# Constant matrix products in idle stretches of TensorE, in an attention and feed-forward kernel

## The chip, the cores and the metric

The kernel runs on one core of a Trainium2 chip. A core has TensorE (PE in the profile) for matrix products, with a queue of weight loads (PEld) beside it, VectorE (DVE), ScalarE (ACT), GpSimd (POOL) and SyncE (SP), which mostly issues DMA transfers. Each engine works off its own instructions in the order in which the program gives them, and waits for others through semaphores. The metric is the device time of one execution in microseconds (us); where several executions were timed, their median.

## The reference

Eight attention heads in each of four batches have 768 positions of width 64. Queries and keys are each assigned to one of 16 centroids of their head, and a query sees only keys of its own cluster. The result of all heads, 3072 rows of 512, goes through a feed-forward layer with a Mish activation.

```python
q_assign = np.argmax(np.einsum('bhsd,hcd->bhsc', q_n, c_n), axis=-1)
k_assign = np.argmax(np.einsum('bhsd,hcd->bhsc', k_n, c_n), axis=-1)
mask = q_assign[:, :, :, None] == k_assign[:, :, None, :]
scores = scale * np.matmul(q, k.transpose(0, 1, 3, 2))
scores = np.where(mask, scores, -1000000000.0)
...
attn = attn / (np.sum(attn, axis=-1, keepdims=True) + 1e-09)
return np.matmul(attn, v).astype(np.float32)
...
h = x @ w_in
g = h * np.tanh(sp)          # sp = log(1 + exp(h))
return (g @ w_out).astype(np.float32)
```

## The kernel before

**Units.** The attention is cut into 96 units: unit i is one head (i // 3 over all batches) and one block of 256 queries. Each unit has two halves a = 0, 1 of 128 queries, and all names carry both: `s12_0` is the score tile of unit 12, first half. Batch 0 is units 0 to 23 and runs in a single-precision form of its own; at the same time the weights of the feed-forward layer are loaded and split into two 16-bit halves (the tiles `w` and `stage`), so that VectorE, ScalarE and GpSimd are busier there than later. From about 175 us on, the feed-forward products of one batch run between the attention of the next.

**One half in batch 0.** `scores` makes s (128 x 768) by four products of width 384 in a tile of two PSUM banks, `[P, 2, 512]`, of which columns 384 to 511 of each bank stay unused: the spare columns. There are two such tiles (the pool `ps2`, tag "S"). `rowmax` reduces s on VectorE to m, `expo` writes p = exp(s + m) on ScalarE with the row sums l, `p_lo` transposes p on TensorE by six products with the identity into two PSUM tiles q, `ptrans` copies these to pt (one by ScalarE, one by VectorE), and `pv` multiplies by the values into o, with the inverse row sums spread by four more products. `pv_out` scales o: ScalarE makes rb, VectorE xf, ScalarE and GpSimd the two halves of x.

**Order.** Nothing is scheduled by the hardware or a compiler. The class `Plan` collects every operation with a time from the tables T and N, sorts them, and issues them in this order; `after` issues first what an operation needs. `tie` then fixes the order of each engine's instructions as issued. Semaphores come from a layer that tracks which instruction reads and writes which tile.

**Other work on TensorE.** `w_sq` makes Gram products of the weights (the tile `gram`, four 128-wide bf16 products per weight tile), `assign_mm` and `assign_put` belong to the centroids. `warm(n)` issues n products of width 512 of the constant tile `idle` (bf16, all ones) into a PSUM tile `wake` that nothing reads. It is called four times: 17 products at the start, 18 and 4 in the assignment of the first heads, and 5 behind the scores of unit 0.

**Operands of a head.** For each head, GpSimd and others prepare A, B, T and Z (`prep_hi`, `prep_lo`), and DMA transfers copy parts between them (`copy_a` and its kin) and put in the cluster rows (`hot_copy`). `scores` waits for the last of these before the first unit of a head.

Of the kernel before, what the change touches and what calls it, by code (L numbers as in the profile page):

```python
# [20 lines left out]
P = 128  # L21
# [50 lines left out]
def tile_clustered_attention_mish_ffn(  # L72
# [9 lines left out]
    nc = tc.nc  # L82
# [22 lines left out]
    pl = Plan(tc)  # L105


    idle = cp.tile([P, 512], BF16, name="idle")
# [3 lines left out]
    def warm(n):  # L112
        for _ in range(n):
            nc.tensor.matmul(wake, idle[:, :P], idle, start=True, stop=True)
# [3 lines left out]
    def share(n, key, late):  # L118

        f = T[key, int(late)]  # L120
        return int((n + 1) * f) != int(n * f)
# [98 lines left out]
    st = {}  # L220
# [387 lines left out]
        eng.dma_start(st["T", n][D : D + NCL].bitcast(F32), stg[r + NCL : r + 2 * NCL])  # L608


    def scores(i, a):
        g, qb, n = units[i]
        pl.after(*((nm, n) for nm in ("hot_copy", "copy_a", "copy_b")))
        q0 = qb * 256 + a * P
        s = ps2.tile([P, 2, 512], F32, tag="S", name=f"s{i}_{a}")
        for j in range(2):
            nc.tensor.matmul(  # L617
                s[:, j, :384], st["B", n][:, q0 : q0 + P], st["A", n][:, j * 384 : (j + 1) * 384],
                start=True, stop=False,
            )  # L620
        for j in range(2):
            nc.tensor.matmul(  # L622
                s[:, j, :384], st["T", n][: D + NCL, q0 : q0 + P],
                st["Z", n][: D + NCL, j * 384 : (j + 1) * 384],
                start=False, stop=True,
            )
        st["s", i, a] = s
        if i == 0 and a:
            warm(5)

    def rowmax(i, a):
        pl.after(("scores", i, a))
# [35 lines left out]
    def mode(i, a):  # L668


        n, late = 2 * i + a, i >= T["units0"]
        if i < T["wide"]:
            return 3
        return 2 if share(n, "f_lo", late) else int(share(n, "f_hi", late))
# [13 lines left out]
    def p_lo(i, a):  # L688
        pl.after(("p_hi", i, a))
        if mode(i, a) == 3:  # L690
            for c in range(6):
                if c % 3 == 0:
                    o = st["q", i, a, c // 3] = ps.tile([P, 512], F32, tag="H", name=f"q{i}_{a}_{c}", bufs=2)
                nc.tensor.transpose(o[:, c % 3 * P : (c % 3 + 1) * P], st["p", i, a][:, c * P : (c + 1) * P], ident)
            return
        t, p, r = st["hl", i, a], st["p", i, a], st["l", i, a]
        if mode(i, a) == 2:
            nc.gpsimd.tensor_scalar(p, p, r, 1.0, op0=ALU.mult, op1=ALU.mult)
            nc.gpsimd.tensor_tensor(t[:, 1], p, t[:, 0], op=ALU.subtract)
        else:  # L700
            nc.vector.scalar_tensor_tensor(t[:, 1], p, r, t[:, 0], op0=ALU.mult, op1=ALU.subtract)  # L701
# [166 lines left out]
    def ffn(j):  # L868
# [3 lines left out]
    ops = {  # L872
        fn.__name__: fn
        for fn in (scores, rowmax, expo, total, recip, p_hi, p_lo, ptrans, e_mish, e_gh, e_gl)
    }
    def start(i):
# [109 lines left out]
    for i in range(NU):  # L986
        for a in range(2):
            if mode(i, a) == 3:
                for key in ("scores", "rowmax", "expo", "recip"):
                    pl.at(start(i) + T[key, a], ops[key], i, a)  # L990
                pl.at(start(i) + T["recip", a] - 0.001, total, i, a)
                pl.at(start(i) + T["q_hi", a], p_hi, i, a)
                pl.at(start(i) + T["q_lo", a], p_lo, i, a)
                pl.at(start(i) + T["q_trans", a], ptrans, i, a)
            else:
                e = i // 2 * 2 + N["E"][i % 2 * 2 + a]
                for key in ("scores", "rowmax", "expo", "total", "recip", "p_hi", "p_lo", "ptrans"):
                    pl.at(e + N[key], ops[key], i, a)
        if i % 2:
            early = mode(i, 0) == 3  # L1000
            for part in range(3):
                pl.at(start(i) + T["pv"] + T["pv_step"] * part if early else i + N["pv"][part], pv, i // 2, part)
            for u in (i - 1, i):
                pl.at(start(i) + T["pv_out"] if early else i + N["pv_out"] + 0.1 * (u - i), pv_out, u)
                pl.at(start(i) + T["pv_out"] if early else i + N["x_lo"] + 0.1 * (u - i), x_lo, u)
# [215 lines left out]
```

## Time and profile before

| | |
|---|---|
| median of 3 executions | 915.11 us (913.28 to 915.86) |
| the profiled execution's own time | 913.7 us |
| its span from the first to the last instruction | 912.0 us |
| mean granted TensorE clock | 0.988 |
| busy: PE, DVE, ACT, POOL | 859.8, 648.3, 490.9, 427.6 us |
| PE busy from 0 to 215 us | 183.73 of 215 us, clock 0.95 |
| PE busy from 215 to 908 us | 675.86 of 693 us, clock 1.00 |
| DVE busy from 0 to 215 us | 175.45 of 215 us |

A row of the timeline gives the start and the busy time in us, engine, line, operation, output and inputs, how many instructions are merged, and in brackets the idle time of the engine just before with what ended it. A row of the table by stage gives a stretch, its length, the busy time of an engine (with its instructions), the granted TensorE clock as a share of full speed, the busy share of the DMA engines and what they moved. Ends of matrix products are modelled, so a step from one start to the next says more about their price than the busy time.

### The profile page before, as it was taken

The page shows a single profiled execution, that of the slowest core. Times are in us where ns is not written, and L with a number is a line of the kernel's source. Part 1 is how long each engine was busy: PE and PEld are TensorE (multiplying, and loading weights), DVE is VectorE, ACT ScalarE, POOL GpSimd, SP SyncE. Part 2 cuts the span into 40 slices and gives each one's busy share as a digit, 9 for nine tenths or more (in the row PEclk, how much of TensorE's full clock was granted, in tenths as well). Part 3 has the DMA queues.
Part 4 walks back from the last instruction along what each step waited for, and adds up shares of the span by engine and source line. Part 5 has one row for each costly group of instructions (what it writes and reads, how often), then busy time and mean ns, then how long its engine had stood idle before and what let it go on. Part 6 is the DMA issues. An engine that isn't in the chain of part 4 may idle for free.

```text
span 912.0 us, 16959 instructions
## 1 busy us (share of the span) xinstructions
PE 859.8 (94%) x6527; PEld 601.3 (66%) x6527; DVE 648.3 (71%) x1083; ACT 490.9 (54%) x833; POOL 427.6 (47%) x424
## 2 busy tenths in 40 slices
PE   7999789879999999999999999999999999999998
PEld 2766566656667667667667666676766776666664
DVE  6879978878988779789987687798977766202110
ACT  5867867646555556555565666465465564111111
POOL 1443638466555554466565445565556543101110
PEclk9999999979999999999999999999999999999999
DMA  8555572258778797589668986779576775000000
GB/s 323 186 171 159 171 225 66 45 106 165 148 144 162 161 209 135 116 160 187 122 132 174 224 162 130 140 140 188 118 144 131 149 131 103 26 12 12 13 13 23
DMA packets 252624, 121.43 MB, mean 133 GB/s; under 512 B 230112, under 2 KB 230112, under 8 KB 252544
## 3 DMA queue, kind: packets, MB, share of 16 engines
q1 hardware_dynamic: 247632, 108.72, 53.7%
q10 hardware_dynamic: 4912, 11.64, 6.0%
q8 instruction: 51, 0.84, 0.4%
q14 instruction: 29, 0.24, 0.1%
HBM read 35.68 MB, written 6.29 MB: 46 GB/s over the span
## 4 chain that ended last, share of the span: by engine, by line
PE 49%; DVE 22%; issue 9%; ACT 8%; POOL 7%; DMA 4%; ACTq 0%; SPq 0%; POOLq 0%; DVEq 0%
DVE m L634 6%; PE o L737 6%; PE h L814 6%; PE h L815 6%; PE h L816 5%; DVE hl L701 5%; PE O L851 5%; PE O L853 5%; PE O L852 5%; PE s L617 4%; DVE g L835 4%; PE s L622 4%; ACT p L646 3%; POOL g L827 2%; DMA pt<-hl 2%
## 5 line engine op out<-in xcount | busy, mean ns | idle before, releaser
L646 ACT ACTIVATE p<-s,m 128x768 f32<-128x768 f32 x192 | 172.9, 901 | 117.1 <-DVE l L658 90.4
L684 POOL TENSOR_SCALAR hl<-p,l 128x768 f16<-128x768 f32 x144 | 160.4, 1119 | 122.8 <-DVE l L666 45.4
L634 DVE TENSOR_REDUCE m<-s 128x1 f32<-128x768 f32 x192 | 182.5, 950 | 32.3 <-PE s L622 29.8
L701 DVE SCALAR_TENSOR_TENSOR hl<-p,l,hl 128x768 f16<-128x768 f32 x144 | 182.5, 1268 | 8.4 <-POOL hl L684 7.8
L827 POOL TENSOR_SCALAR g<-u,mscg 128x512 f16<-128x512 f32 x96 | 83.9, 875 | 222.2 <-ACT u L823 193.1
L814 PE MATMUL h<-x,w 128*128 128x256 f16 x640 | 177.2, 277 | 3.2 <-ACT u L823 3.0
L815 PE MATMUL h<-x,w 128*128 128x256 f16 x640 | 175.8, 275 | 0.0
L816 PE MATMUL h<-x,w 128*128 128x256 f16 x640 | 175.7, 275 | 0.0
L835 DVE SCALAR_TENSOR_TENSOR g<-u,mscg,g 128x512 f16<-128x512 f32 x96 | 95.3, 994 | 98.2 <-POOL g L827 95.8
L853 PE MATMUL O<-w,g 128*128 128x512 f16 x384 | 145.7, 379 | 7.6 <-DVE g L835 7.6
L851 PE MATMUL O<-w,g 128*128 128x512 f16 x384 | 146.0, 380 | 3.6 <-POOL g L827 2.7
L852 PE MATMUL O<-w,g 128*128 128x512 f16 x384 | 145.5, 379 | 0.0
L617 PE MATMUL s<-A,B 128*128 128x384 f32 x384 | 123.8, 404 | 15.6 <-ACT p L646 11.6
L823 ACT ACTIVATE u<-h,msch 128x512 f32<-128x512 f32 x96 | 65.5, 683 | 80.8 <-PE h L816 80.1
L622 PE MATMUL s<-Z,T 80*128 80x384 f32 x384 | 101.0, 345 | 0.5 <-DMA T<-stg 0.5
L814 PEld LDWEIGHTS <-w 128*128 128x128 f16 x768 | 75.6, 98 | 33.3 <-issue 22.0
L617 PEld LDWEIGHTS s<-A,B 128*128 128x128 f32 x384 | 64.1, 195 | 39.8 <-ACT p L646 20.9
L646 ACT ACT_TABLE_LOAD x35 | 44.9, 1283 | 78.1 <-DVE m L634 70.9
L815 PEld LDWEIGHTS <-w 128*128 128x128 f16 x768 | 76.0, 99 | 14.8 <-issue 3.5
L816 PEld LDWEIGHTS <-w 128*128 128x128 f16 x768 | 75.6, 98 | 9.1
L737 PE MATMUL o<-pt,v 128*64 128x256 f16 x1296 | 78.0, 274 | 0.5 <-DVE l L658 0.5
L737 PEld LDWEIGHTS <-v 128*64 128x64 f16 x1296 | 67.8, 110 | 15.5 <-issue 11.6
(179 smaller groups left out, 1167.2 us busy)
## 6 DMA issues: line engine op xcount, KB each, us to landing
qk<-in_qk_dram SPq DMA_DIRECT2D x32, 384.0 KB, 5.1
stage<-in_w_in_dram SPq DMA_DIRECT2D x16, 512.0 KB, 8.0
stage<-in_w_out_dram SPq DMA_DIRECT2D x16, 512.0 KB, 4.9
vraw<-in_vP_dram SPq DMA_DIRECT2D x16, 384.0 KB, 6.3
out_dram<-osb SPq DMA_DIRECT2D x24, 256.0 KB, 4.3
T<-A ACTq DMA_DIRECT2D x30, 192.0 KB, 3.3
Z<-B SPq DMA_DIRECT2D x30, 192.0 KB, 3.3
B<-T ACTq DMA_DIRECT2D x28, 192.0 KB, 3.6
```

The source lines that it names most:

```text
L617: nc.tensor.matmul(s[:, j, :384], st["B", n][:, q0 : q0 + P], st["A", n][:, j * 384 : (j + 1) * 384], start=True, stop=False,)
L634: nc.vector.tensor_reduce(m, st["s", i, a][:, :, :384], axis=AX.XY, op=ALU.max, negate=True)
L646: nc.scalar.activation(p.rearrange("p (n x) -> p n x", n=2), st["s", i, a][:, :, :384], AF.Exp, bias=st["m", i, a], scale=1.0, accum_out=l,)
L684: nc.gpsimd.tensor_scalar(t[:, 0], p, r, 1.0, op0=ALU.mult, op1=ALU.mult)
L701: nc.vector.scalar_tensor_tensor(t[:, 1], p, r, t[:, 0], op0=ALU.mult, op1=ALU.subtract)
L737: nc.tensor.matmul(o[s * D : s * D + D, :256], v if early else v[:, int(part == 1)], st["pt", 2 * m + s][:, :, c + (0 if early or part < 2 ...
L814: nc.tensor.matmul(o, wh, xh, start=(c == 0), stop=False)
L815: nc.tensor.matmul(o, wh, xl, start=False, stop=False)
L816: nc.tensor.matmul(o, wl, xh, start=False, stop=(c == 3))
L851: nc.tensor.matmul(o, gh, wh, start=(f == 0 and fi == 0), stop=False)
L852: nc.tensor.matmul(o, gh, wl, start=False, stop=False)
L853: nc.tensor.matmul(o, gl, wh, start=False, stop=(f == 7 and fi == 1))
```

## The change

A new helper `nap(i, a, n)` issues n products of width 128 of the constant tile `idle` into the spare columns of the second bank of score tile s{i}_{a}. Nothing reads them. It is called at three places: 22 products into s9_1 ahead of the scores of unit 10, 22 into s11_1 ahead of those of unit 12, and 12 into s17_0 ahead of the transposes of unit 16's second half; at the last place the scores s17_0 are asked for first, which were ahead of it already. The call `warm(5)` behind the scores of unit 0 becomes `warm(18)`. That is 69 products more; no operation is removed, and no other one changes its place on any engine.

```diff
+    def nap(i, a, n):
+
+        o = st["s", i, a][:, 1, 384:]
+        for _ in range(n):
+            nc.tensor.matmul(o, idle[:, :P], idle[:, :P], start=True, stop=True, skip_group_check=True)
+
     def scores(i, a):
         g, qb, n = units[i]
         pl.after(*((nm, n) for nm in ("hot_copy", "copy_a", "copy_b")))
+        if (i, a) in ((10, 0), (12, 0)):
+            nap(i - 1, 1, 22)
         q0 = qb * 256 + a * P
         s = ps2.tile([P, 2, 512], F32, tag="S", name=f"s{i}_{a}")
...
         if i == 0 and a:
-            warm(5)
+            warm(18)
...
     def p_lo(i, a):
         pl.after(("p_hi", i, a))
         if mode(i, a) == 3:
+            if (i, a) == (16, 1):
+                pl.after(("scores", 17, 0))
+                nap(17, 0, 12)
             for c in range(6):
```

The instructions of PE at the three later places follow, with what each waits for in brackets (the semaphore of an engine; Activation is ScalarE). The numbers behind a name's last underscore count tiles and mean nothing here. First, ahead of the scores of unit 10, before:

```order
L694 MATMUL q9_0_3_1012<-ident_128,p9_0_995 128x128 [waits DVE_49]
L694 MATMUL q9_0_3_1012<-ident_128,p9_0_995 128x128 x2
L617 MATMUL s10_0_1047<-A_3_768,B_3_781 128x384 [waits DVE_49]
L617 MATMUL s10_0_1047<-A_3_768,B_3_781 128x384
L622 MATMUL s10_0_1047<-Z_3_783,T_3_771 128x384 x2
L694 MATMUL q9_1_0_1059<-ident_128,p9_1_1038 128x128 [waits PE_49,Activation_49]
```

and with the change, of the 22 pairs of weight load and product the first and the last:

```order
L705 MATMUL q9_0_3_1025<-ident_128,p9_0_1008 128x128 x2
L615 LDWEIGHTS idle_108
L615 MATMUL s9_1_1011<-idle_108 128x128 [waits Activation_49]
...
L615 MATMUL s9_1_1011<-idle_108 128x128
L625 MATMUL s10_0_1082<-A_3_781,B_3_794 128x384 [waits DVE_49]
L625 MATMUL s10_0_1082<-A_3_781,B_3_794 128x384
L630 MATMUL s10_0_1082<-Z_3_796,T_3_784 128x384 x2
L705 MATMUL q9_1_0_1094<-ident_128,p9_1_1051 128x128 [waits PE_49]
```

The wait for ScalarE, whose semaphore value is the one that the exponential p9_1 sets, stood at the transposes of p9_1 behind the scores s10_0. It now stands at the first constant product, ahead of s10_0. Second, ahead of the scores of unit 12, before:

```order
L694 MATMUL q11_0_3_1178<-ident_128,p11_0_1154 128x128 [waits DVE_49]
L694 MATMUL q11_0_3_1178<-ident_128,p11_0_1154 128x128 x2
L617 MATMUL s12_0_1201<-A_4_1028,B_4_1042 128x384 [waits DMAHW5_49,DMAHW3_49,Pool_49]
L617 MATMUL s12_0_1201<-A_4_1028,B_4_1042 128x384
L622 MATMUL s12_0_1201<-Z_4_1044,T_4_1031 128x384 [waits DMAHW6_49,DMAHW4_49,DMAHW2_49]
L694 MATMUL q11_1_0_1214<-ident_128,p11_1_1199 128x128 [waits PE_49,Activation_49]
```

and with the change:

```order
L705 MATMUL q11_0_3_1213<-ident_128,p11_0_1189 128x128 x2
L615 LDWEIGHTS idle_108
L615 MATMUL s11_1_1192<-idle_108 128x128 [waits Activation_49]
...
L615 MATMUL s11_1_1192<-idle_108 128x128
L625 MATMUL s12_0_1258<-A_4_1041,B_4_1055 128x384 [waits DMAHW5_49,DMAHW3_49,Pool_49]
L630 MATMUL s12_0_1258<-Z_4_1057,T_4_1044 128x384 [waits DMAHW6_49,DMAHW4_49,DMAHW2_49]
L705 MATMUL q11_1_0_1271<-ident_128,p11_1_1234 128x128 [waits PE_49]
```

Here too the wait for ScalarE, now for p11_1, has moved from behind the scores s12_0 to ahead of them. At the third place the first product waits for VectorE's row maximum m17_0, and the transposes q16_1 behind it keep their own wait for p16_1:

```order
L290 MATMUL gram16_1121<-w15_1593 128x128
L615 LDWEIGHTS idle_108
L615 MATMUL s17_0_1653<-idle_108 128x128 [waits DVE_49]
...
L615 MATMUL s17_0_1653<-idle_108 128x128
L705 MATMUL q16_1_0_1686<-ident_128,p16_1_1650 128x128 [waits PE_49,Activation_49]
```

Before, the transposes stood directly behind the Gram products there.

## The prediction

> **What bounds the kernel now.** I read the page first. Nearly all of the span is TensorE at full clock; its holes lie in the first quarter, where the change is, so I went on by stage.
>
> ```profile
> span 912.0 us, 16959 instructions
> PEclk9999999979999999999999999999999999999999
> ```
>
> The table by stage for PE, with cuts at the moments where the clock changes. The clock column is 1.00 or 0.50 and a mean of both where it changes within a stretch.
>
> ```profile
> 23.25:23.50 0.25, 0.25 (x3) 0.81 0.00 0
> 95.00:95.25 0.25, 0.25 (x3) 0.67 0.00 0
> 98.25:98.50 0.25, 0.25 (x4) 0.51 0.73 229
> 129.00:129.25 0.25, 0.01 (x1) 0.93 1.05 406
> 19.99:23.40 3.41, 0.26 (x2) 1.00 0.41 150
> 78.02:81.43 3.41, 1.66 (x12) 1.00 0.39 87
> 91.67:95.08 3.41, 1.44 (x8) 1.00 0.61 158
> 125.80:129.21 3.41, 1.37 (x13) 1.00 1.02 353
> ```
>
> A mean of 0.81 means full clock for 62% of that quarter: the cut is at 23.40. Likewise 95.08, 129.21, and the return at 98.50. The distances are 71.68 = 21 x 3.413, 34.13 = 10 x 3.413, and 3.42: the clock is decided on a fixed grid of 3.41 us. The last four rows are grid windows. Those with 0.26, 1.44 and 1.37 us of PE work were followed by half clock, the one with 1.66 us was not. So the limit lies between 1.44 and 1.66 us, and of the four places that get products three were followed by a cut; the one ahead of unit 10 was not.
>
> A cut costs only where TensorE sets the pace. Three rows by stage (the first two with PE, PEld, DVE, ACT and POOL in this order, the third PE alone) say who does:
>
> ```profile
> 22.09:28.53 6.44, 5.05 (x28) 4.48 (x28) 4.61 (x8) 6.38 (x13) 1.85 (x3) 0.74 0.47 157
> 80.80:91.67 10.87, 10.87 (x88) 1.00 0.76 207
> 91.42:106.30 14.88, 12.03 (x81) 8.23 (x79) 14.80 (x19) 11.15 (x20) 11.02 (x10) 0.89 0.56 166
> ```
>
> In the first cut stretch ScalarE works 6.38 of 6.44 us; from 80.80 to 91.67 TensorE works without a gap; from 91.42 to 106.30, over the second cut, VectorE works 14.80 of 14.88 us. What is late on TensorE in the middle stage, or reaches VectorE in the last, is late for all.
>
> **18 in place of 5 behind the first scores.** Rows of PE and ACT:
>
> ```profile
> 10.36 4.06 PE L114 MATMUL wake<-idle 128*128 128x512 bf16 x18
> 18.27 1.25 PE L114 MATMUL wake<-idle 128*128 128x512 bf16 x5
> 24.12 0.99 PE L617 MATMUL s<-A,B 128*128 128x384 f32 x2
> 25.79 0.96 DVE L634 TENSOR_REDUCE m<-s 128x1 f32<-128x768 f32 x1 [0.72 <-PE s L622]
> 29.16 0.48 ACT L715 COPY pt<-q 128x384 f32<-128x384 f32 x1 [0.64 <-PE q L694]
> 29.80 0.90 ACT L646 ACTIVATE p<-s,m 128x768 f32<-128x768 f32 x1 [0.16 <-DVE m L634]
> ```
>
> One product of 512 columns costs 4.06 / 18 = 0.226 us, thirteen more 2.93, so they end at 22.45. The next work starts 0.26 us before 23.40, at 23.14, so nothing is delayed, and the window to 23.40 holds 2.7 us of work: no cut. The gain on TensorE would be half of 3.41, 1.7 us. But ScalarE is full until 28.53 and takes nothing earlier. What is left is the 0.16 us which the exponential at 29.80 waited for the row maximum. Term: **-0.16**, bounds -1.7 and 0.
>
> **22 products ahead of unit 10.** The price of a product of width 128 is read from the Gram products (same width and type), by steps from start to start. How long after a ScalarE start TensorE goes on is read from the last pair:
>
> ```profile
> 87.14 0.86 PE L290 MATMUL gram<-w 128*128 128x128 bf16 x12
> 87.84 0.82 PE L694 MATMUL q<-ident,p 128*128 128x128 f32 x6
> 25.55 1.08 PE L290 MATMUL gram<-w 128*128 128x128 bf16 x8
> 26.39 0.79 PE L617 MATMUL s<-A,B 128*128 128x384 f32 x2
> 79.73 0.90 ACT L646 ACTIVATE p<-s,m 128x768 f32<-128x768 f32 x1 [0.49 <-DVE m L634]
> 80.80 0.62 PE L617 MATMUL s<-A,B 128*128 128x384 f32 x2 [1.75 <-DVE stg L596]
> 81.82 0.96 DVE L634 TENSOR_REDUCE m<-s 128x1 f32<-128x768 f32 x1
> 128.19 0.91 ACT L646 ACTIVATE p<-s,m 128x768 f32<-128x768 f32 x1
> 129.24 1.54 PE L694 MATMUL q<-ident,p 128*128 128x128 f32 x6 [2.07 <-ACT p L646]
> ```
>
> Full clock: (87.84 - 87.14) / 12 = 0.058 us; half clock: (26.39 - 25.55) / 8 = 0.105. By the order, the first product waits for p9_1, which starts at 79.73; with 129.24 - 128.19 = 1.05 the products start at 80.78. The hole from 79.05 to 80.80 is over by then: they fill none of it, and stand ahead of s10_0 with 22 x 0.058 = 1.28. So s10_0 starts at 82.06, 1.26 late. Queued behind it is the gapless stretch, and at its end ScalarE's rb and VectorE's xf, for which all that follows waits. Carried: **+1.26**, with 0 and 1.3 as bounds.
>
> **22 products ahead of unit 12.**
>
> ```profile
> 90.80 0.87 PE L694 MATMUL q<-ident,p 128*128 128x128 f32 x6
> 93.65 0.59 PE L617 MATMUL s<-A,B 128*128 128x384 f32 x2 [1.97 <-DMA A<-A]
> 93.54 0.91 ACT L646 ACTIVATE p<-s,m 128x768 f32<-128x768 f32 x1
> 93.30 1.28 DVE L341 SCALAR_TENSOR_TENSOR w<-w,ws0r,w 128x1024 f16<-128x1024 f32 x1
> 94.97 0.95 DVE L634 TENSOR_REDUCE m<-s 128x1 f32<-128x768 f32 x1
> 96.97 1.67 DVE L341 SCALAR_TENSOR_TENSOR w<-w,ws0r,w 128x1024 f16<-128x1024 f32 x1
> ```
>
> Before, s12_0 started at 93.65, as its operands landed. Now the products wait for p11_1. That was at 93.54 and is at 94.80 with the 1.26, so they start at 95.85, and TensorE is idle from 92.93 (91.67 + 1.26): 2.92 us in place of 1.98. On the same grid the window to 95.08 holds 1.26 us of work, under 1.44: the cut comes, and the products run at half clock, 22 x 0.105 = 2.31, to 98.16. At half clock the row maximum came 25.79 - 24.12 = 1.67 after its scores, so m12_0 starts at 99.83 and not at 94.97: **+4.86**, which includes the 1.26. Without a cut it is 95.85 + 1.28 + (81.82 - 80.80) = 98.15: +3.18. VectorE, full in this stage, has m12_0 ahead of the weight work and m12_1, and stands still meanwhile. Some comes back: the weight step at 96.97 took 1.67 beside GpSimd's operand work, the like one at 93.30 only 1.28, and GpSimd is but 1.26 late and will be ahead of it. I take **-0.6** for this and the weight steps behind it, bounds -1.0 and 0.
>
> **12 products ahead of q16_1.**
>
> ```profile
> 126.45 0.95 DVE L634 TENSOR_REDUCE m<-s 128x1 f32<-128x768 f32 x1
> 124.24 0.88 PE L694 MATMUL q<-ident,p 128*128 128x128 f32 x6
> 125.75 1.08 PE L737 MATMUL o<-pt,vraw 128*64 128x256 f32 x8
> 132.44 1.15 PE L737 MATMUL o<-pt,vraw 128*64 128x256 f32 x8
> ```
>
> Here the wait is early: m17_0 ends at 127.40, the products at 127.40 + 12 x 0.058 = 128.1, and q16_1 comes only at 129.24, so they cost nothing. The window to 129.21 then holds 1.37 + 0.70 = 2.07 us, over 1.66: no cut. Transposes, scores and four Gram products to the next o took 132.44 - 129.24 = 3.20 at half clock; at full clock 125.75 - 124.24 = 1.51 and 4 x 0.058 = 0.23, 1.74 together. ScalarE had waited before and feeds from these results: **-1.46**, and 0 if the grid lies so that the hole was not cut.
>
> The page "TensorE: Matmul & The Clock Gate" of the Trainium skill, in its section "Why this matters for your kernels", asks for no idle gap over some 3 us. By this rule the hole of 2.07 us would need no products, and their term would be 0 and not -1.46. This trace cuts the clock there, so the row decides. Its Part 1 calls the window free-running, of 3413 ns. The grid above agrees, and no run shown here tells whether another execution has the same phase.
>
> **The sum.** -0.16 + 4.86 - 0.6 - 1.46 = **+2.64** on the profiled execution's 913.7 us, 916.3. That execution is 1.4 under the median of 915.11, so on the median it is 917.75. With the grid so that neither hole ahead of unit 12 nor the one ahead of q16_1 is cut it is -0.16 + 3.18 - 0.6 = +2.42; the mixed cases give +0.96 and +4.1. From 215 us on TensorE is busy 675.86 of 693 us, so a delay there has nowhere to go. I forecast **917.6 us**, with 916.1 to 919.2 as its own range. What a measurement of this kernel can tell from no change is about 0.3%, 2.75 us, which cuts this range in the middle.
>
> **Rivals.**
>
> *The clock is what counts.* TensorE sets the pace in the cut stretches, the products end all three cuts and wait for nothing that matters: -1.7 - 1.7 - 1.46 = -4.9, 910.2 us. For it speaks that VectorE waited 0.72 us for the slow scores at 25.79. Against it are the two full engines above and the place of the waits. Chance 0.11.
>
> *The delay is given back.* ScalarE stood 2.80 us in front of unit 16 for a transfer:
>
> ```profile
> 127.82 0.48 ACT L715 COPY pt<-q 128x384 f32<-128x384 f32 x1 [2.80 <-DMA Z<-B]
> ```
>
> If the transfer keeps its time, 2.8 of the +4.1 that arrive are absorbed and -1.46 follows: about 0, 915 us. Against it: the transfer is issued behind GpSimd's B, which waits for sums of ScalarE, so it should come later as well. Chance 0.15.
>
> *A second window at half clock.* The cut ahead of unit 12 lasts on:
>
> ```profile
> 197.48:200.89 3.41, 2.95 (x11) 0.50 0.76 144
> ```
>
> This window with 0.46 us idle was not enough to bring the clock back. The one from 95.08 would have 0.77 idle. Then scores, transposes and values to 101.9 run at half speed too, up to 1.7 more, 919.4. VectorE's full queue hides part of that. Chance 0.12.
>
> **Chances.** The forecast has 0.62, split in half by the 0.3%. Slower by over 0.3%: 0.31 + 0.12 = 0.43. Within 0.3%: 0.31 + 0.15 and a little of the first rival, 0.47. Faster: 0.10. The range of 912.9 to 920.6 leaves out the first rival and the far end of the last.
>
> **What would show it.** No half clock at 23 to 27 us and none at 129 to 133; the first product at s9_1 within 0.1 us of its exponential's end; s10_0 some 1.2 us later behind stg; TensorE idle for 2.9 us ahead of the products at s11_1, and VectorE waiting for s12_0 where it had waited for nothing. If the products at s9_1 or s11_1 start as the hole opens, or s12_0 comes no later than 2 us behind, counted against VectorE's weight steps, the forecast is wrong.

## The result, and the profile after

| | before | after |
|---|---|---|
| median of 4 executions each | 914.19 us (911.69 to 915.86) | 924.96 us (919.32 to 927.31) |
| ratio | | 1.0101, interval 1.007 to 1.0132 |
| the profiled execution: its own time, its span | 913.7, 912.0 us | 919.32, 917.6 us |
| mean granted clock in it | 0.988 | 0.992 |

The change makes the kernel slower by 1.0%. That is outside the predicted range (912.9 to 920.6), though its sign has the forecast's side. The granted clock is higher than before, so the time was not lost to the clock. The profiled execution of after is the fastest of its four; 5.6 us of span separate the two profiles. Among the experiments below, one execution of e8_one (3019 us) and one of e10_pad (2208 us) ran far slower than all others and are in no ratio.

The places of the change come first. Timeline of the kernel after: TensorE and VectorE at the first scores, ahead of unit 10 and ahead of unit 12, then TensorE and ScalarE at unit 16. L615 is the product in the spare columns, L625 and L630 the scores, L705 the transposes, L642 the row maximum.

```profile
18.35 4.06 PE L114 MATMUL wake<-idle 128*128 128x512 bf16 x18
23.24 0.88 PE L705 MATMUL q<-ident,p 128*128 128x128 f32 x6 [0.83 <-ACT p L654]
...
80.64 1.39 PE L615 MATMUL s<-idle 128*128 128x128 bf16 x22 [1.73 <-ACT p L654]
81.84 0.60 PE L625 MATMUL s<-A,B 128*128 128x384 f32 x2
...
95.92 1.44 PE L615 MATMUL s<-idle 128*128 128x128 bf16 x22 [2.91 <-ACT p L654]
97.12 0.99 PE L625 MATMUL s<-A,B 128*128 128x384 f32 x2
98.79 0.96 DVE L642 TENSOR_REDUCE m<-s 128x1 f32<-128x768 f32 x1 [2.40 <-PE s L630]
...
132.70 0.83 PE L615 MATMUL s<-idle 128*128 128x128 bf16 x12
133.37 0.82 PE L705 MATMUL q<-ident,p 128*128 128x128 f32 x6
131.46 0.48 ACT L726 COPY pt<-q 128x384 f32<-128x384 f32 x1 [0.98 <-PE s L630]
```

The waits came as the working said. The products at s9_1 start behind the exponential and fill nothing of the hole; those at s11_1 stand behind 2.91 us of idle (2.92 in the working), and VectorE then waits 2.40 us for s12_0. Ahead of unit 16 there is no hole left to fill: the products are followed at once by the transposes, and behind them TensorE works on.

What was not in the working is seen when the start of each row maximum is compared with the one in the profile of before. The lag is +2.82 us at unit 24, the end of batch 0; it grows to +3.42 at unit 42's first half, +5.08 at its second, +6.43 at unit 66's second half, and is +5.63 at unit 95. Half of the loss arises where the change does nothing at all. PE from 215 us on agrees; the prediction had 675.86 of 693 us for before, which is 17.1 us of idle, and after has 21.2:

```profile
215.00:910.00 695.00, 673.82 (x5206) 1.00 0.64 125
```

At unit 42 it is GpSimd that waits. It makes hl, the 16-bit halves of p, which DMA transposes then carry into pt; the buffer of hl is free again when a transpose has read it. Its rows in before and in after:

```profile
321.00 0.90 POOL L684 TENSOR_SCALAR hl<-p,l 128x768 f16<-128x768 f32 x1
325.17 0.90 POOL L684 TENSOR_SCALAR hl<-p,l 128x768 f16<-128x768 f32 x1 [3.27 <-DMA pt<-hl]
```

```profile
324.41 0.91 POOL L692 TENSOR_SCALAR hl<-p,l 128x768 f16<-128x768 f32 x1
330.25 0.90 POOL L692 TENSOR_SCALAR hl<-p,l 128x768 f16<-128x768 f32 x1 [4.93 <-DMA pt<-hl]
```

1.66 us more: this is the step of the lag from +3.42 to +5.08.

### The profile page after: what moved, and what is told of

The parts are those of the page before. It is cut to its first block, busy times and chain, and to the rows that moved or that the text cites. A ratio compares the mean times of both kernels' runs of the same rounds, so it can differ in the third digit from the quotient of the medians.

```text
span 917.6 us, 17095 instructions
## 1 busy us (share of the span) xinstructions
PE 861.7 (94%) x6594; PEld 602.9 (66%) x6596; DVE 649.1 (71%) x1083; ACT 491.6 (54%) x833; POOL 425.4 (46%) x424
## 3 DMA queue, kind: packets, MB, share of 16 engines
q1 hardware_dynamic: 247632, 108.72, 55.5%
## 4 chain that ended last, share of the span: by engine, by line
PE 49%; DVE 21%; issue 9%; ACT 8%; POOL 7%; DMA 5%; ACTq 0%; SPq 0%; POOLq 0%; DVEq 0%
PE h L825 6%; PE h L826 6%; PE h L827 6%; DVE m L642 6%; PE O L864 6%; PE O L862 6%; PE O L863 5%; DVE hl L712 5%; PE o L748 5%; PE s L625 4%; PE s L630 4%; DVE g L846 3%; ACT p L654 3%; DMA pt<-hl 3%; POOL g L838 2%
## 5 line engine op out<-in xcount | busy, mean ns | idle before, releaser
L642 DVE TENSOR_REDUCE m<-s 128x1 f32<-128x768 f32 x192 | 182.4, 950 | 36.2 <-PE s L630 33.0
L625 PE MATMUL s<-A,B 128*128 128x384 f32 x384 | 123.2, 402 | 16.2 <-ACT p L654 15.2
L630 PE MATMUL s<-Z,T 80*128 80x384 f32 x384 | 100.1, 342 | 0.5 <-DMA T<-stg 0.4
L825 PEld LDWEIGHTS <-w 128*128 128x128 f16 x768 | 75.5, 98 | 33.0 <-issue 21.6
L625 PEld LDWEIGHTS s<-A,B 128*128 128x128 f32 x384 | 63.5, 193 | 40.1 <-ACT p L654 24.6
```

Of the source, the lines that this page charges most:

```text
L625: nc.tensor.matmul(s[:, j, :384], st["B", n][:, q0 : q0 + P], st["A", n][:, j * 384 : (j + 1) * 384], start=True, stop=False,)
L642: nc.vector.tensor_reduce(m, st["s", i, a][:, :, :384], axis=AX.XY, op=ALU.max, negate=True)
L825: nc.tensor.matmul(o, wh, xh, start=(c == 0), stop=False)
```

## The experiments

Every ratio is to the kernel before on the same chip. The first four do one part of the change alone.

**e1_warm.** `warm(18)`, no `nap`.

```diff
-            warm(5)
+            warm(18)
```

> Only the 18 products in place of 5 behind the first scores. Two questions for all four parts: how late is batch 0 at its end (the row maximum of unit 24's first half, against the kernel before), and how late is the end of the program. Theory W (the waits): what a part does to batch 0 is what it does to the end. Here: no half clock at 23 to 27 us, batch 0 0.2 to 0.4 us early, the end the same, 0 to -0.4 us. Theory S (the later stage): from unit 24 on the waits for transfers shift whenever batch 0 shifts, by an amount that batch 0's delay does not tell. Then the end can be 2 to 6 us off although batch 0 is not late.

915.47 us against 915.57, ratio 1.0 (0.9977 to 1.0024). Within some 2 us the 13 products cost and bring nothing; a term of -0.16 can't be told from 0 here.

**e2_unit10.** Only the 22 products ahead of unit 10.

```diff
+        if (i, a) == (10, 0):
+            nap(i - 1, 1, 22)
```

> Only the 22 products ahead of unit 10. Theory W: they start 1.05 us after the exponential p9_1 does, scores of unit 10 are 1.25 us late, the whole of batch 0 0.9 to 1.4 us late, the end +1.0 to +1.4 us. Theory S: batch 0 the same +0.9 to +1.4, the end +2 to +8 us.

916.47 us, ratio 1.0019 (0.9999 to 1.004): +0.9 us by the medians, +1.7 by the ratio.

**e3_unit12.** Only the 22 products ahead of unit 12.

```diff
+        if (i, a) == (12, 0):
+            nap(i - 1, 1, 22)
```

> Only the 22 products ahead of unit 12. Theory W: they start behind the exponential p11_1 at 94.6 us, not as the hole opens at 91.7; scores of unit 12 are 2.2 us late (1.28 us of products and about 1 us of wait), 3.3 if the clock is cut in the hole of 2.9 us; the end of batch 0 +1.5 to +2.5 us, and the end of the program the same. Theory S: the end +3 to +8 us with the same batch 0.

918.5 us, ratio 1.0027 (1.0007 to 1.0046). By the medians +2.9, by the ratio +2.5.

**e4_unit16.** Only the 12 products ahead of q16_1.

```diff
+            if (i, a) == (16, 1):
+                pl.after(("scores", 17, 0))
+                nap(17, 0, 12)
```

> Only the 12 products ahead of the transposes of unit 16's second half. Theory W: they run from 127.4 to 128.1 us in the hole, no half clock at 129 to 133 us, batch 0 1.2 to 1.5 us early against the profile before where that hole was cut, the end -0.5 to -1.5 us. Theory S: batch 0 the same, the end anywhere from -2 to +5 us.

915.49 us, ratio 1.0009 (0.9991 to 1.0026). No gain in time, where theory W had 0.5 to 1.5 us. By the ratios, the four parts add up to 1.0055, about +5 us. By its ratio the whole change is at +9, so the next four kernels took it apart from the other side.

**e5_gram.** All 69 products; the later three groups go to spare columns of the Gram tile, and so wait for no exponential.

```diff
-        o = st["s", i, a][:, 1, 384:]
+        o = st["gram"][:, 256:384]
```

> All 69 added products at the same places, but those of the three later places go into columns 256 to 383 of the Gram product's tile, which only TensorE writes there, so that they wait for no other engine. Theory W (the waits cost, the products do not): they start as the holes open, at about 79.1, 91.7 and 127.2 us, are over before the hole ends, and the scores of units 10 and 12 come as before; the holes ahead of unit 12 and of unit 16's transposes are no longer cut; the end -0.5 to -2 us. Rival P (more TensorE work in this stage costs as such, or through the transfers later): +4 to +9 us, as with the change.

920.33 us, ratio 1.005 (1.0035 to 1.0066). It has no delay at units 10 to 14 and is still 4.6 us slower. So the waits are not the whole story; the theory that they are fell here.

**e6_again.** The change once more, beside e5, e7 and e8.

> The change itself once more, for its size beside the others of this call. The four parts alone gave 0, +1.7, +2.5 and +0.8 us. If they add up, +4 to +6 us; if the parts raise each other, +8 to +10 us, as in the four executions first seen.

922.81 us, ratio 1.0071 (1.0044 to 1.0098): +7.1 us by the medians, between the two ranges expected.

**e7_both.** The 22 products ahead of units 10 and 12, nothing else.

```diff
+        if (i, a) in ((10, 0), (12, 0)):
+            nap(i - 1, 1, 22)
```

> The products ahead of units 10 and 12 together, without the other two parts. Theory W: the delay of the first is carried into the start of the second, so +1.25 and then +1 of wait and +1.25 to +2.3 of products: +3.5 to +4.8 us. Theory A (they raise each other through the longer hole): +6 us or more.

920.93 us, ratio 1.005 (1.0034 to 1.0066): +4.6 us by the ratio, +5.2 by the medians, near the upper end of theory W.

**e8_one.** As e7, one product in place of 22: the wait without the products.

```diff
-            nap(i - 1, 1, 22)
+            nap(i - 1, 1, 1)
```

> One product in place of 22 ahead of units 10 and 12, without the other two parts: the moved wait stays, the products are gone. Theory W: ahead of unit 10 the wait ends when the other one did, so it costs nothing; ahead of unit 12 the scores wait for the exponential until 94.6 us and not for the transfer until 93.65, so they are 1 us late; the end +0.3 to +1.2 us. If the products set the price and the wait does not, 0.

917.14 us, ratio 1.0005 (0.9988 to 1.0022). The same waits without the number of products cost half a microsecond by the ratio (1.4 by the medians), and the products without the waits (e5) cost 4.6. What e5, e6 and e7 share, and e8 lacks, is a number of added instructions.

**What this led to.** The profile's DMA part has two queues called "instruction"; q8 is the larger. Its page row says 51 packets before and 52 after, 16 KB each. PE's rows say whose they are: before, 6527 matrix products and 6527 weight loads were recorded, 13054 / 51 = 256 to a packet; and from one packet to the next lie 253 of them on average. Rows of the page of after and of e9_gram_full (below):

```profile
PE 861.7 (94%) x6594; PEld 602.9 (66%) x6596; DVE 649.1 (71%) x1083; ACT 491.6 (54%) x833; POOL 425.4 (46%) x424
q1 hardware_dynamic: 247632, 108.72, 55.5%
q8 instruction: 52, 0.85, 0.4%
```

```profile
PE 860.8 (94%) x6655; PEld 604.2 (66%) x6655; DVE 651.7 (71%) x1083; ACT 491.4 (54%) x833; POOL 427.1 (47%) x424
q1 hardware_dynamic: 247632, 108.72, 53.7%
```

A load thus sits at a fixed place in TensorE's instructions. The change adds some 137 of them, half a block, and from then on every load comes half a block, about 9 us, from where it came before. Theory L: the moved loads fall among DMA transposes and hold them up. It says that the number of added instructions decides, not where they stand or what they wait for: half a block costs, and a whole block (256) costs nothing, since the loads are back in their old places. The three kernels that follow pad TensorE's instructions with small products of width 128 where it has nothing to do.

**e9_gram_full.** e5 padded to a whole block: 60 small products in place of the 13 wide ones, 12 more in unit 5.

```diff
             warm(5)
+            pad(wake[:, :P], 60)
...
+            if (i, a) == (5, 1):
+                pl.after(("scores", 6, 0))
+                pad(st["gram"][:, 256:384], 12)
```

> All three later groups of products in the spare columns of the Gram tile (so they wait for no exponential), as in e5_gram, but with small products added where TensorE has nothing to do (behind the first scores, and ahead of transposes in unit 5), so that TensorE's instruction stream grows by 257 and not by 137: one whole 16 KB block of instructions. The instruction loads of the q8 queue then fall after unit 17 where they fall before the change. Theory L (moved instruction loads meet the DMA transposes from unit 42 on): no loss behind unit 24, -1 to +1 us against the kernel before, and loads at units 41.6, 43.6, 65.6, 67.6. Rival (the products themselves, or a disturbed batch 0, cost time later): +4 to +5 us as in e5_gram, wherever the loads fall.

914.59 us against 915.49, ratio 0.9975 (0.9958 to 0.9991). With 59 products more than e5, it is 5.7 us faster than that by the medians, and a little faster than the kernel before.

**e10_pad.** The kernel before with half a block of padding, and nothing of the change.

```diff
             warm(5)
+            pad(wake[:, :P], 57)
...
+            if (i, a) == (5, 1):
+                pl.after(("scores", 6, 0))
+                pad(st["gram"][:, 256:384], 12)
```

> The kernel before with none of the change's products, but with 69 small products of width 128 in two places where TensorE has nothing to do (57 behind the first scores, 12 ahead of transposes in unit 5): TensorE's instruction stream grows by 139, as with the change (137). No waits, nothing late in batch 0. Theory L: the loads fall at units 42.0 and 66.0 as with the change, and GpSimd waits longer for the DMA transposes there: +3 to +5 us from unit 24 to the end. Rival (delay of batch 0, waits or products of the later groups are the cause): 0, within 1 us.

921.38 us against 915.49, ratio 1.0056 (1.0035 to 1.0077). On the same chip e9, which has padding at the same two places (60 and 12 products) and 56 products more, takes 6.8 us less.

**e11_change_full.** The change, with its waits, padded to a whole block as in e9.

```diff
-            warm(18)
+            warm(5)
+            pad(wake[:, :P], 60)
...
+            if (i, a) == (5, 1):
+                pl.after(("scores", 6, 0))
+                pad(st["gram"][:, 256:384], 12)
```

> The change with its waits (spare columns of the score tile), with the same padding as e9_gram_full: TensorE's stream grows by 255. Theory L: only the delay of batch 0 is left, +2.5 to +4 us by unit 24 and as much at the end. Rival: +6 to +9 us as the change.

916.81 us, ratio 1.0006 (0.9986 to 1.0026): 6.0 us faster than the change in e6. The +1.3 us by the medians is less than the 2.5 to 4 expected; against e9, which differs from it in the waits alone, it is +2.2.

**e12_pad_again.** e10 once more, for its profile.

> The kernel of e10_pad once more, for its profile (the profiled execution of e10_pad ran with TensorE at under half speed throughout and its stages can't be compared). Theory L: +4 to +7 us in time; no delay against other executions of the kernel before up to unit 24; at unit 42 a 16 KB load of the q8 queue lies among the DMA transposes pt<-hl, their packets stop for about the time that it takes (1.1 us), GpSimd waits 4.5 to 5.5 us for pt<-hl ahead of its hl (3.27 before), and the row maxima are 1.5 to 2.3 us later behind that place; the same at unit 66. Rival (the padding costs where it stands): the row maxima are late by 3 us or more already at unit 24, and keep that lag.

919.77 us against 915.17, ratio 1.005 (1.0032 to 1.0068). In its profile, below, GpSimd's wait at unit 42 is as expected (4.68 us); the row maxima step by 1.41 us there at once and by 1.27 at unit 66, somewhat less than the 1.5 to 2.3 expected.

Three pairs now differ in the length of the stream, and each has its half block 4.6 to 6.0 us behind: e5 and e9 by 5.7, the change (e6) and e11 by 6.0, the padded kernel and the one before by 5.9 and 4.6. In two of the pairs the one with more products is the faster one.

The profiles say where. Start of the row maximum against the profile of before, in us. (That profile is ahead of most others by some 1.2 us at unit 5, so the steps down a column count, not its level. The level at unit 24 in particular is that of one execution: e6_again, the kernel of after, has +4.58 there.)

| unit, half | e12_pad_again | e9_gram_full | e11_change_full | after | e5_gram |
|---|---|---|---|---|---|
| 5, first | +1.16 | +1.01 | +1.75 | -0.37 | +1.12 |
| 12, first | +1.31 | +1.36 | +5.10 | +3.82 | +1.31 |
| 24, first | +0.63 | +0.98 | +4.30 | +2.82 | +2.55 |
| 42, first | -0.15 | +0.22 | +4.98 | +3.42 | +2.56 |
| 48, first | +2.80 | +0.92 | +5.27 | +5.08 | +6.21 |
| 66, first | +2.68 | +0.83 | +5.27 | +5.47 | +6.08 |
| 66, second | +3.95 | +0.78 | +5.24 | +6.43 | +7.68 |
| 95, first | +3.16 | +0.12 | +4.53 | +5.63 | +7.20 |
| added to TensorE's stream | half | whole | whole | half | half |
| loads near units 42 and 66 fall at | 42.0, 66.0 | 41.6, 65.6 | 41.6, 65.6 | 42.0, 65.9 | 42.1, 66.0 |

The last row counts in units by the row maxima; before has 41.6 and 65.6. The half block steps up at unit 42, by 1.7 to 3.7 us (1.5 in e6_again), and again at unit 66, by 1.0 to 1.6; the whole block by 0.7 and 0.3 at most in the first place, and not at all in the second. From unit 24 to unit 95 the half block loses 2.5 (e12), 2.8 (after), 4.3 (e6_again) and 4.7 us (e5), the whole block -0.9 (e9) and +0.2 (e11). The page's rows for q1 above agree: the same 247632 packets of the kernel's own transfers take 55.5% of the engines' time in after and 53.7% in e9, although e9 is the shorter one.

A rival would be that TensorE itself waits for its instructions. The waits of TensorE from 200 to 905 us don't show it: all of its idle time there ends with another engine. What grows most is the wait of the scores for ScalarE's p, 7.3 us in before, 8.0 in e9 and 12.9 in after.

The clock has a part in the size of the step. In e12 a hole on TensorE behind unit 42 left 1.10 us of work in a window of 3.41 us, and the next window ran at half clock; e5 had the same with 0.52 us, from 336.35 us on, and after had not, with 1.67. Of e12's step of 2.95 us, 1.41 come at once, and the rest lies between units 43 and 45, where this half clock falls. Table by stage of e12, for PE:

```profile
329.70:333.11 3.41, 1.10 (x11) 1.00 1.00 186
333.11:336.52 3.41, 3.41 (x14) 0.50 0.98 227
```

The packets show how the steps come about. DMA queues of after in the stretch from 327.2 to 328.4 us (packets, MB, share of 16 engines' time), then the table by stage around it with GpSimd's busy time, the clock, the DMA share and GB/s, and then the same for before, where the same transposes run:

```profile
q1 hardware_dynamic: 585, 0.15, 207.8%
q8 instruction: 1, 0.02, 5.8%
...
326.50:327.00 0.50, 0.00 (x0) 1.00 1.07 130
327.00:327.50 0.50, 0.00 (x0) 1.00 1.24 269
327.50:328.00 0.50, 0.00 (x0) 1.00 4.25 134
328.00:328.50 0.50, 0.00 (x0) 1.00 0.03 3
328.50:329.00 0.50, 0.00 (x0) 1.00 0.09 10
329.00:329.50 0.50, 0.00 (x0) 1.00 0.76 161
329.50:330.00 0.50, 0.00 (x0) 1.00 1.28 291
```

```profile
323.00:323.50 0.50, 0.00 (x0) 1.00 1.28 175
323.50:324.00 0.50, 0.00 (x0) 1.00 1.27 288
324.00:324.50 0.50, 0.00 (x0) 1.00 1.28 284
324.50:325.00 0.50, 0.00 (x0) 1.00 1.28 268
```

The load takes 1.11 us, from 327.24 on. The packets under way then take many times as long (a share of 4.25: their times add up to over four times what 16 engines have, so they overlap and stand in line), and for a microsecond almost nothing moves. e12, with none of the change in it, has the same stop (table by stage, all engines PE, PEld, DVE, ACT and POOL; its load runs from 323.54 for 1.11 us), and GpSimd waits longer there; e9 waits less:

```profile
324.00:324.50 0.50, 0.50 (x4) 0.23 (x3) 0.50 (x1) 0.00 (x0) 0.00 (x0) 1.00 3.06 19
324.50:325.00 0.50, 0.50 (x4) 0.19 (x2) 0.29 (x1) 0.14 (x1) 0.00 (x0) 1.00 0.07 7
325.00:325.50 0.50, 0.50 (x4) 0.45 (x3) 0.00 (x0) 0.50 (x1) 0.00 (x0) 1.00 0.08 9
...
326.43 0.90 POOL L689 TENSOR_SCALAR hl<-p,l 128x768 f16<-128x768 f32 x1 [4.68 <-DMA pt<-hl]
```

```profile
326.08 0.91 POOL L697 TENSOR_SCALAR hl<-p,l 128x768 f16<-128x768 f32 x1 [3.96 <-DMA pt<-hl]
```

Not every load holds something up. That of before at 317.07, which takes 1.21 us, falls among large packets, and from 316.9 to 318.4 the queue beside it is as full as ever:

```profile
q1 hardware_dynamic: 148, 0.40, 93.8%
q8 instruction: 1, 0.02, 5.1%
```

Nor is before free of such stops. Its load at 678.5 us, among 256-byte packets too, is followed by one (table by stage with GpSimd's busy time):

```profile
679.00:679.50 0.50, 0.41 (x1) 1.00 1.68 17
679.50:680.00 0.50, 0.00 (x0) 1.00 0.08 8
```

What this one costs, if anything, was not measured. At units 42 and 66 GpSimd waits for the transposes: at unit 66 for 2.63 us in before, 2.58 in e9, 3.88 in e12 and 3.58 in after.

The Trainium skill, page "Runtime: NRT & Kernel Launch", section "Instruction fetch mechanics", says that instructions are fetched in blocks of 16 KiB, 256 instructions, over a DMA queue of the sequencer's own, and that crossing a block's end is "mostly hidden". The blocks agree with the trace (13054 / 51 = 256). That they are hidden agrees with TensorE's waits above, but not with the transposes beside them: padding alone costs 4.6 and 5.9 us.

Three things stay open. The profile of e12 loses 2.5 us from unit 24 to the end, while the medians differ by 4.6 and 5.9; that profile is the fastest execution of e12 (915.1 us of span), the other half-block profiles lose up to 4.7 us, and what a median execution of e12 loses, and where, was not seen. The records don't name the DMA engine of a packet, so whether the load stands ahead of transpose packets on one engine, and all others wait for that one, was not settled. And e7, which adds a third of a block, is 3.8 us slower than e8 by the medians, and its profile doesn't show why: it is +5.28 at unit 24, but e8's is +7.14 there, in an execution of 920.77 us that is 3.6 above e8's median. So the lag of batch 0 in one profile can't be put down to a change by itself.

## Why the prediction was wrong

**The sign** held, and the mechanism at the first three places; the term of the fourth was not found, and the size failed by a term that was missing.

*The limit of the clock.* The windows of 3.41 us are there. Table by stage of after, for PE:

```profile
93.71:97.12 3.41, 1.20 (x22) 1.00 0.50 143
97.00:97.25 0.25, 0.25 (x7) 0.75 0.00 0
100.50:100.75 0.25, 0.25 (x3) 0.92 0.00 0
114.00:114.25 0.25, 0.25 (x5) 0.89 1.06 209
110.78:114.19 3.41, 1.79 (x16) 1.00 0.21 45
```

The clock was cut at 97.12 (0.75 is full clock for half of the quarter), was back at 100.54, and was cut again at 114.19, five windows behind the first cut. The window ahead of 97.12 has 1.20 us of PE work, which fits a limit between 1.44 and 1.66. The window ahead of 114.19 has 1.79 and was cut all the same, so the limit is not as sharp as the prediction read it from its rows. The grid's phase was assumed to be that of before, and is not: 97.12 - 23.40 = 73.72 is 21.6 windows. It is not a matter of the kernel: e6_again, the same kernel as after, was cut at 98.79 and 115.86, half a window later.

*18 in place of 5, -0.16.* The mechanism was right. In all six profiles with 5 products behind the first scores (before, e2, e3, e4, e7, e8) the clock was cut between 21.4 and 24.7 us, and in none of the seven with 18 or more; yet the ratio in e1 is 1.0, within some 2 us on either side, which is too coarse for the size.

*22 ahead of unit 10, +1.26.* Right: from unit 9 to unit 10 the lag grows by 1.14 in after, 1.13 in e6 and 1.14 in e11. Alone it cost +1.7 in time by the ratio, with an interval from -0.1 to 3.7.

*22 ahead of unit 12, +4.86 less 0.6.* Right in the mechanism, too large by about a microsecond. The idle time of 2.92 was 2.91. The lag at m12_0 was +3.82 and not +4.86, or +3.95 counted from the -0.13 that the profile had at unit 9; with another phase of the grid the cut came at 97.12, behind the products, not ahead of them. They ran 1.20 us and not 2.31, and the scores and transposes behind them at half speed. In e7 and e11 no cut fell near unit 12, and there the lag grows by 3.28 and 3.21 from unit 9; the working has 3.18 for that case.

*12 ahead of q16_1, -1.46.* Not found. In e4, which has only these, time didn't fall (1.0009, interval 0.9991 to 1.0026). In the profile of e4 the transposes run at full clock and the lag falls by 1.32 from unit 14 to unit 24, but without any product there it falls by 0.69 in e12 and by 2.94 in e3. The term was priced from a cut that belongs to one execution: of the seven profiles without products at this place, these transposes ran at half clock in two (cuts at 129.22 in before and 131.22 in e1). The prediction named the other case, with 0, but put the whole -1.46 into the sum. In after, the wait of ScalarE that kept this hole open (2.80 us for the transfer of Z) was gone, and q16_1 had no idle time ahead of it.

*The sum, +2.64.* For batch 0 it comes close: +2.82 at unit 24 in after, and the waits alone, e11 against e9, make 2.2 us in the medians. That is luck in part: the term of unit 12 was too large and the gain at unit 16 was not found, and the same kernel has +4.58 at unit 24 in e6. As the whole change of the kernel it is wrong by its missing term. The failed step is the sentence before the forecast, "From 215 us on TensorE is busy 675.86 of 693 us, so a delay there has nowhere to go". The delay indeed had nowhere to go: e11 carries it from unit 42 (+4.98) to unit 95 (+4.53). But the sentence was taken to mean that nothing new arises behind 215 us, and the 137 added instructions were priced only where they stand. They shifted the loads of TensorE's instructions against the DMA transposes of the later batches (steps are seen at units 42 and 66, none in the last batch). By the pairs of kernels above, the shift costs 4.6 to 6.0 us, more than all the terms of the sum; 2.5 to 4.7 us of it are seen behind unit 24 in the profiles.

*The rivals.* "The clock is what counts" fell: the mean clock rose to 0.992 and the time rose too. What it would have brought without the waits may be seen in e9 (0.9975), though its padding is in that number as well. "The delay is given back" came about in part: ScalarE's 2.80 us ahead of unit 16 went to 0.98, and yet the lag at unit 24 was +2.82. "A second window at half clock" didn't come: the clock was back at 100.54.

## What to carry to other kernels

Count the instructions that a change adds to an engine as well as their time: every 256 of TensorE's were one 16 KB load here, and an added half block moves every later load against all later transfers. Take a clock cut for a chance, not a certainty, when it is priced from one execution: the grid lies elsewhere in the next. Where a change in one place seems to cost time in a later one, compare the places of the "instruction" queue's packets with the small-packet transfers there, and pad the engine's stream to a whole block as a control before blaming the change. An idle stretch can be filled only by work that waits for nothing later than the stretch's beginning: a spare corner of a tile brings along the waits of that tile.

## What the runs showed of the hardware that was not expected

Behind one instruction load of 1.11 us among DMA transposes of 256-byte packets, 269 GB/s fell to 3 to 10 for about a microsecond, while one among packets of about 3 KB left 277 GB/s. Half a block (138) of added TensorE instructions made the whole kernel 0.5% slower, a whole block (256) did not. And the grid of 3.41 us on which the clock is decided has no fixed phase to the start of the program: the cuts of after, at 97.12 and 114.19 us, are not on the grid of before, and those of e6_again, the same kernel, at 98.79 and 115.86 us, are not on that of after.
